# Attention and two expert layers: GpSimd makes part of the first operands, and a tile takes one reciprocal

## The chip, the core and the metric

The kernel runs on one core of one Trainium2 chip, as one program. The metric is the time of an execution on the device in microseconds (us). The engines are named as the profile names them: PE is TensorE (PEld its weight loads), DVE is VectorE, ACT is ScalarE, POOL is GpSimd, SP is SyncE, which here issues all the DMAs.

## What is computed

Local attention in chunks of 32 queries, then two layers of experts over the 1536 x 512 result. The first layer weighs its 4 experts by normalized `domain_probs`; the second weighs its 8 by gate logits that go through eight row and column normalizations.

```python
def _attn_ref(q, k, v, mem_k, mem_v):          # B, H, S, D = 2, 8, 768, 64
    for c in range(nc):                        # chunks of 32 queries
        k_full = np.concatenate([mem_k, k_ctx], axis=2)      # 8 + up to 56 keys
        scores = scale * np.matmul(q_c, k_full.transpose(0, 1, 3, 2))
        scores = scores - np.max(scores, axis=-1, keepdims=True)
        a = np.exp(scores)
        a = a / (np.sum(a, axis=-1, keepdims=True) + 1e-09)
        out[:, :, c_start:c_end] = np.matmul(a, v_full)

def _moe_ref(x, domain_probs, w1, w2):         # 1536 x 512, 4 experts of 1024
    for e in range(E):
        h = np.maximum(x @ w1[e], 0.0)
        out += p[:, e:e + 1] * (h @ w2[e])
# _moe2_ref: the same with 8 experts and the normalized gate table P
```

## The kernel before

**Tiles and operands.** Attention goes over 12 tiles of 128 tokens. The expert layers go over 36 units, an expert times a block of 512 tokens (`sb`, four tiles). Each matrix product is done by a scheme of seven products on half-size blocks (`PRODUCTS`: M1 to M7): the first operands are blocks A11, A12, A22 and combinations S1 to S4, the second ones B11, B21, B22 and T1 to T4. Every operand is kept as a pair of float16 halves, a high one (ACT converts) and a low one (DVE subtracts the high half from the source), and a product of 12 matmuls multiplies three pairs of halves.

**Where the work comes from.** `prepare` (L262) makes operands: it adds and subtracts 128 x 512 float32 sources on DVE (L299), has ACT convert to the high half (L307), and DVE make the low half (L311). `prep_w` (L323) loads four blocks of a weight and calls it; the first expert's weights are prepared as `w10`, `w11` (W1, groups 0 and 1) and `w20`, `w21` (W2) while attention runs, their sources lying in `raw`, `acc` and `h1` buffers. After every fourth attention tile `prepare` makes the operands `x0`, `x1`, `x2` of that block from the transposed output. `layer1` (L499) runs seven products, and DVE and ACT combine their results (L525, L531, L554) and make the operands h of the second layer: high halves on ACT (L539), low halves on DVE (L544 with the rectifier, L547 without). `layer2` (L571) runs seven products for each of two row groups and adds them into `acc` (L608, L612).

**An attention tile.** `scores` (L393): 32 small matmuls into two banks, one for each of two halves (`par`); DVE takes the maximum of each half (L419). In a wide tile DVE subtracts it (L424) and ACT takes one exponential of both halves (L440); in the two other tiles DVE scales the maximum (L421) and ACT takes eight exponentials with it as bias (L431). `weighted` (L443): transposes (L375), a copy by ACT (L381), 32 matmuls with the values, whose last column gives the sum; then for each half DVE adds 1e-9 (L469), takes the reciprocal (L470) and multiplies (L471); transposes again, and ACT copies into `raw`.

**What sets the order.** All operations are recorded in `Program` with the engine, an assumed cost and the keys that they read and write. `run` (L86) plays them through a list scheduler with these costs and due times (numbers in `PLAN`, L17), and emits every engine's instructions in the order found. Each engine then works strictly in that order and waits on semaphores. Where the planner sees PE idle early on, it puts filler matmuls (`warm`, L706). In the plan before, POOL has only the set-up of `ident` and `ones`.

Of the kernel before, what the change touches and what calls it, by code (L numbers as in the profile page):

```python
# [10 lines left out]
F32 = mybir.dt.float32  # L11
# [2 lines left out]
AX = mybir.AxisListType  # L14

P = 128
PLAN = dict(rf=(0.0, 4.0, 5.6, 18.0), wide=(0, 1, 2, 3, 4, 5, 7, 9, 10, 11), lead=27.37, step=6.0, pace=1.0, early=4.11, behind=3.0, tr=0.11, sm=0.04, margin=0.59, marg0=0.1, marga=0.12, margs=1.0, slack=1.13, slacka=0.35, slack0=0.29, mm=0.1088)  # L17


class Op:  # L20
# [154 lines left out]
def tile_attention_moe_moe(  # L175
# [52 lines left out]
    def f32t(tag, name="f"):  # L228
        return buf(tag, [P, 512], F32, name)
# [93 lines left out]
    def prep_w(which, e, g, src=None, temps=("T0", "T1"), force=None):  # L323
# [42 lines left out]
    def small(tag):  # L366
        return smt[tag]
# [25 lines left out]
    def scores(i):  # L393
# [19 lines left out]
        scale = 1.0 / float(D) ** 0.5  # L413
        eks = (f"{et}0", f"{et}1")
        wide = i in PLAN["wide"]
        for par in range(2):
            def mx(par=par):
                sm = small(st)
                nc.vector.tensor_reduce(out=sm[:, 0, :, par], in_=sb4(par), axis=AX.X, op=ALU.max)  # L419
                if not wide:  # L420
                    nc.vector.tensor_scalar_mul(sm[:, 0, :, par], sm[:, 0, :, par], -scale)  # L421

            def sub(par=par):
                nc.vector.tensor_tensor(  # L424
                    out=ex(et)[:, :, par, :], in0=sb4(par),
                    in1=small(st)[:, 0, :, par, None].to_broadcast([P, HP, 64]), op=ALU.subtract)

            def expf(par=par):
                sm = small(st)
                for hp in range(HP):  # L430
                    nc.scalar.activation(out=ex(et)[:, hp, par, :], in_=sb4(par)[:, hp, :], func=AF.Exp,  # L431
                                         scale=scale, bias=sm[:, 0, hp, par, None])

            pg.add("DVE", dve(256) + (0.0 if wide else 0.1), mx, (sc[par],), (f"{st}m{par}",))
            if wide:
                pg.add("DVE", dve(256), sub, (sc[par], f"{st}m{par}"), (eks[par],))
            else:
                pg.add("ACT", HP * 0.22, expf, (sc[par], f"{st}m{par}"), (eks[par],))
        if wide:
            pg.add("ACT", act(512, False), lambda: nc.scalar.activation(  # L440
                out=ex(et), in_=ex(et), func=AF.Exp, scale=scale), (), eks)

    def weighted(i, xdst):  # L443
        et, at, st = ee_t[i % 2], aT_t[i % 2], f"sm{i % 2}"
# [18 lines left out]
                            start=True, stop=True, skip_group_check=True)  # L463

        pg.add("PE", 32 * PLAN["sm"], go, (at, v0, v1), nb)
        for par in range(2):
            def norm(par=par):
                s = small(st)[:, 1, :, par]
                nc.vector.tensor_scalar_add(s, nb4(par)[:, :, D], 1e-9)  # L469
                nc.vector.reciprocal(s, s)  # L470
                nc.vector.tensor_tensor(  # L471
                    out=ex(et)[:, :, par, :], in0=nb4(par)[:, :, :D],
                    in1=s[:, :, None].to_broadcast([P, HP, D]), op=ALU.mult)

            pg.add("DVE", dve(256) + 0.2, norm, (nb[par],), (f"{st}s{par}", f"{et}{par}"))
# [22 lines left out]

    def layer1(sb, g, hs):  # L499
        bk = {"A": f"1A{blocks['1'] % 2 if blocks['1'] >= 4 else 0}", "B": "1B", "C": "1C"}  # L500
        blocks["1"] += 1
        last = {}
        for name, a, b, bb, first in PRODUCTS:
            bn, xt, wt = bk[bb], xtag(sb, a), f"w1{g}{b}"

# [28 lines left out]

        def hilo(o, s, rect):
            d = f"{hs}{o}"

            def hi():
                nc.scalar.activation(out=pair(d)[:, 0], in_=v2(f32t(s)), func=AF.Relu if rect else AF.Copy)  # L539

            def lo():
                t = pair(d)
                if rect:
                    nc.vector.scalar_tensor_tensor(out=t[:, 1], in0=v2(f32t(s)), scalar=0.0, in1=t[:, 0],  # L544
                                                   op0=ALU.max, op1=ALU.subtract)
# [198 lines left out]
    for gt in range(NT):  # L744
# [7 lines left out]
        if gt == 3:  # L752
            raw1 = [f"raw1{i}" for i in range(4)]
            h1 = [f"h1{o}" for o in OPA]
            prep_w(W1, 0, 0, raw1, force=PLAN["rf"][0])
            prep_w(W1, 0, 1, [f"acc{i}" for i in range(4)], ("acc4", "acc5"), force=PLAN["rf"][1])
            prep_w(W2, 0, 0, h1[:4], h1[4:6], force=PLAN["rf"][2])
            prep_w(W2, 0, 1, raw1, force=PLAN["rf"][3])
# [154 lines left out]
```

## Time and profile before

| | |
|---|---|
| Median of 3 runs | 1410.34 us (1410.24 to 1411.14) |
| The profiled execution | 1410.84 us |
| Its span, first to last instruction | 1409.1 us |
| PE busy | 1390.9 us, 99% |
| DVE busy | 1223.4 us, 87% |
| ACT busy | 720.6 us, 51% |
| POOL busy | 0.8 us |
| Mean granted TensorE clock | 0.999 of full speed |
| DMA | 71.47 MB, mean 51 GB/s |

The shares are means over the program. The attention stage and the preparation of the first operands lie in its first 130 us; the rest is the run of expert products. Matmuls are pipelined and their ends modelled, so a busy PE isn't PE at its peak, and the span on POOL is rough. A duration in the timeline includes the drain of an instruction, which the next one's start overlaps; the distance between starts is what an instruction costs its engine when they stand back to back.

### The profile page before, as it was taken

Reading aid. Unit: us, or ns where it says so; the run is one execution under the profiler, and the core shown is the slowest. Engines: PE = TensorE matmul, PEld = TensorE weight load, DVE = VectorE, ACT = ScalarE, POOL = GpSimd, SP = SyncE. Lnnn points to the kernel's source line nnn. Section 1 sums busy time; section 2 is a strip of 40 time slices with the busy share of each in tenths; the row PEclk is TensorE's granted clock in tenths of the full one; section 3 lists DMA queues with packets and bytes.
Section 4 is the critical chain, followed back from the end, with each engine's and each line's share of the span. In section 5 each row is a group of like instructions: output and inputs, shape, how many; then the busy total and the mean of one; then the engine's idle time right before and its main releaser. Section 6 shows DMA issues by size and latency. Waiting matters only on the chain.

```text
span 1409.1 us, 32996 instructions
## 1 busy us (share of the span) xinstructions
PE 1390.9 (99%) x14119; PEld 1244.0 (88%) x14119; DVE 1223.4 (87%) x2274; ACT 720.6 (51%) x1297; POOL 0.8 (0%) x7
## 2 busy tenths in 40 slices
PE   8899999999999999999999999999999999999998
PEld 8778888888889998888888888888888888888887
DVE  6998986996997999999899699699789789889874
ACT  4757564453554566556445445345356356445540
POOL 0000000000000000000000000000000000000000
PEclk9999999999999999999999999999999999999999
DMA  9620210120110111112012012012011111110001
GB/s 332 198 77 31 61 61 9 46 69 9 39 38 9 31 53 46 31 46 69 9 46 68 9 46 69 9 41 69 6 46 46 31 39 38 46 35 28 17 16 61
DMA packets 64819, 71.47 MB, mean 51 GB/s; under 512 B 6304, under 2 KB 55456, under 8 KB 64672
## 3 DMA queue, kind: packets, MB, share of 16 engines
q1 hardware_dynamic: 64672, 69.36, 15.8%
q8 instruction: 110, 1.80, 0.5%
q14 instruction: 37, 0.30, 0.1%
HBM read 66.20 MB, written 3.15 MB: 49 GB/s over the span
## 4 chain that ended last, share of the span: by engine, by line
PE 86%; DVE 11%; ACT 1%; issue 1%; DMA 0%; POOLq 0%; POOL 0%; SPq 0%; ACTq 0%
PE bank1A L493 24%; PE bank2A L493 24%; PE bank1C L493 12%; PE bank2C L493 12%; PE bank1B L493 6%; PE bank2B L493 6%; DVE t_f L525 1%; PE bank1A L706 1%; DVE b_f L554 1%; DVE raw_f L299 1%; DVE T_f L299 1%; DVE x2A_exp L471 1%; DVE h0S_op L547 0%; DVE acc_f L612 0%; DVE h0A_op L544 0%
## 5 line engine op out<-in xcount | busy, mean ns | idle before, releaser
L381 ACT ACTIVATE s_f<-bank1A 128x512 f32<-128x512 f32 x216 | 127.2, 589 | 258.1 <-PE bank1A L493 241.3
L493 PEld LDWEIGHTS <-w10T_op 128*128 128x128 f16 x1728 | 168.8, 98 | 22.3 <-issue 2.5
L493 PEld LDWEIGHTS <-w11T_op 128*128 128x128 f16 x1728 | 169.0, 98 | 20.0 <-issue 0.4
L493 PEld LDWEIGHTS <-w10B_op 128*128 128x128 f16 x1296 | 126.7, 98 | 15.5 <-issue 0.9
L493 PEld LDWEIGHTS <-w11B_op 128*128 128x128 f16 x1296 | 126.7, 98 | 15.5 <-issue 0.8
L493 PEld LDWEIGHTS <-h0S_op 128*128 128x128 f16 x1152 | 112.6, 98 | 14.4 <-issue 1.4
L493 PEld LDWEIGHTS <-h1S_op 128*128 128x128 f16 x1152 | 112.7, 98 | 13.1
L612 DVE SCALAR_TENSOR_TENSOR acc_f<-bank2A,pr,acc_f 128x256 f32<-128x256 f32 x168 | 80.8, 481 | 44.5 <-PE bank2A L493 44.5
L493 PEld LDWEIGHTS <-h2S_op 128*128 128x128 f16 x1104 | 108.0, 98 | 12.5
L525 DVE SCALAR_TENSOR_TENSOR t_f<-bank1C,s_f 128x512 f32<-128x512 f32 x144 | 98.7, 686 | 14.6 <-PE bank1C L493 13.3
L493 PEld LDWEIGHTS <-h0A_op 128*128 128x128 f16 x864 | 84.4, 98 | 10.1 <-issue 0.2
L493 PEld LDWEIGHTS <-h1A_op 128*128 128x128 f16 x864 | 84.5, 98 | 9.8
L493 PEld LDWEIGHTS <-h2A_op 128*128 128x128 f16 x828 | 81.0, 98 | 9.4
L539 ACT ACTIVATE h1A_op<-t_f 128x512 f16<-128x512 f32 x72 | 45.1, 629 | 59.3 <-DVE t_f L525 56.9
L539 ACT ACTIVATE h2A_op<-t_f 128x512 f16<-128x512 f32 x69 | 43.1, 625 | 30.2 <-DVE t_f L525 30.2
L539 ACT ACTIVATE h0A_op<-t_f 128x512 f16<-128x512 f32 x72 | 45.1, 629 | 24.0 <-DVE t_f L525 23.9
L612 DVE SCALAR_TENSOR_TENSOR acc_f<-bank2C,pr,acc_f 128x256 f32<-128x256 f32 x84 | 40.4, 481 | 19.2 <-PE bank2C L493 19.1
L544 DVE SCALAR_TENSOR_TENSOR h1A_op<-t_f,h1A_op 128x512 f16<-128x512 f32 x72 | 48.4, 687 | 7.8 <-ACT h1A_op L539 7.0
L525 DVE SCALAR_TENSOR_TENSOR t_f<-bank1B,s_f 128x512 f32<-128x512 f32 x72 | 49.4, 686 | 5.5 <-PE bank1B L493 5.3
L531 ACT ACTIVATE a_f<-bank1A 128x512 f32<-128x512 f32 x72 | 42.8, 594 | 20.5 <-PE bank1A L493 19.3
L554 DVE SCALAR_TENSOR_TENSOR b_f<-t_f,b_f 128x512 f32<-128x512 f32 x72 | 49.6, 689 | 1.7
L554 DVE SCALAR_TENSOR_TENSOR b_f<-t_f,a_f 128x512 f32<-128x512 f32 x72 | 49.4, 686 | 0.5 <-ACT a_f L531 0.5
(329 smaller groups left out, 3162.7 us busy)
## 6 DMA issues: line engine op xcount, KB each, us to landing
raw_f<-in_moe_w_dram SPq DMA_DIRECT2D x184, 256.0 KB, 2.8
out_dram<-acc_f SPq DMA_DIRECT2D x12, 256.0 KB, 2.0
acc_val<-in_v_dram SPq DMA_DIRECT2D x8, 260.0 KB, 5.2
h2A_val<-in_v_dram SPq DMA_DIRECT2D x8, 260.0 KB, 4.8
x2S_key<-in_k_dram SPq DMA_DIRECT2D x8, 256.0 KB, 4.8
acc_key<-in_k_dram SPq DMA_DIRECT2D x8, 256.0 KB, 4.9
h2S_val<-in_v_dram SPq DMA_DIRECT2D x6, 260.0 KB, 4.8
h2S_key<-in_k_dram SPq DMA_DIRECT2D x6, 256.0 KB, 5.3
```

The source lines that it names most:

```text
L299: nc.vector.tensor_tensor(out=f32t(o), in0=f32t(a), in1=f32t(b), op=alu)
L381: nc.scalar.activation(out=dst(), in_=src(), func=AF.Copy, scale=scale)
L471: nc.vector.tensor_tensor(out=ex(et)[:, :, par, :], in0=nb4(par)[:, :, :D], in1=s[:, :, None].to_broadcast([P, HP, D]), op=ALU.mult)
L493: nc.tensor.matmul(o, lhsT=l, rhs=r, start=st, stop=sp, skip_group_check=True)
L525: nc.vector.scalar_tensor_tensor(out=f32t(d), in0=bank[rb], scalar=CL1, in1=f32t(s), op0=ALU.mult, op1=ALU.add)
L531: nc.scalar.activation(out=f32t("a21"), in_=bank[bn], func=AF.Relu, scale=CL1)
L539: nc.scalar.activation(out=pair(d)[:, 0], in_=v2(f32t(s)), func=AF.Relu if rect else AF.Copy)
L544: nc.vector.scalar_tensor_tensor(out=t[:, 1], in0=v2(f32t(s)), scalar=0.0, in1=t[:, 0], op0=ALU.max, op1=ALU.subtract)
L554: nc.vector.scalar_tensor_tensor(out=f32t(o), in0=f32t(t), scalar=0.0, in1=f32t(s), op0=ALU.max, op1=alu, reverse1=rev)
L612: nc.vector.scalar_tensor_tensor(out=o, in0=s, scalar=sc, in1=o, op0=ALU.mult, op1=ALU.add)
L706: nc.tensor.matmul(bank["1A1"][:, :P], lhsT=ones, rhs=ones, start=True, stop=True)
```

## The change

- `prepare` takes an engine for its adds and one for its low halves. POOL makes the adds and subtracts for `w11`, `w20`, `w21`, `x0` and `x1`, and the low halves of `x1` and `x2`. For a low half on POOL `tensor_tensor` takes the place of `scalar_tensor_tensor` (the scale is 1 there). `layer1` gives POOL the low half of S4 in its blocks 0, 1, 2 and 6.
- The sums of both halves of an attention tile go into one small tile; one reciprocal over eight columns serves both, and the multiplication of each half waits for it.
- Both maxima of a tile share one key (`m`) of the planner, and in a tile that isn't wide one scaling serves both.
- The numbers in `PLAN` are others: which tiles are wide, when the weights are loaded, the lead of the first products, the margins.

```diff
-PLAN = dict(rf=(0.0, 4.0, 5.6, 18.0), wide=(0, 1, 2, 3, 4, 5, 7, 9, 10, 11), lead=27.37, step=6.0, pace=1.0, early=4.11, behind=3.0, tr=0.11, sm=0.04, margin=0.59, marg0=0.1, marga=0.12, margs=1.0, slack=1.13, slacka=0.35, slack0=0.29, mm=0.1088)
+PLAN = dict(rf=(0.0, 4.0, 42.7, 18.0), wide=(0, 1, 2, 4, 5, 6, 7, 8, 10, 11), lead=29.35, step=11.93, pace=1.0, early=3.15, behind=5.1, tr=0.11, sm=0.04, pw=(0, 1, 1, 1), px=((1, 0), (1, 1), (0, 1)), ph=((0, 'S4'), (1, 'S4'), (2, 'S4'), (6, 'S4')), margin=0.39, marg0=0.2, marga=0.07, margs=1.0, slack=1.15, slacka=0.43, slack0=0.3, mm=0.1088)
...
+def gps(n):
+    return 0.1 + n / 480.0
...
-    smt = {f"sm{i}": pool.tile([P, 2, HP, 2], F32, tag=f"sm{i}", name=f"sm{i}") for i in range(2)}
+    smt = {f"sm{i}": pool.tile([P, 2, 2, HP], F32, tag=f"sm{i}", name=f"sm{i}") for i in range(2)}
...
-    def prepare(dst, kind, scale, src, temps=("T0", "T1")):
+    def prepare(dst, kind, scale, src, temps=("T0", "T1"), adder="DVE", low="DVE"):
...
-                    nc.vector.tensor_tensor(out=f32t(o), in0=f32t(a), in1=f32t(b), op=alu)
-
-                pg.add("DVE", dve(512), go, (a, b), (o,))
+                    e = nc.gpsimd if adder == "POOL" else nc.vector
+                    e.tensor_tensor(out=f32t(o), in0=f32t(a), in1=f32t(b), op=alu)
+
+                pg.add(adder, gps(512) if adder == "POOL" else dve(512), go, (a, b), (o,))
...
+                    if low == "POOL":
+                        assert scale == 1.0
+                        nc.gpsimd.tensor_tensor(out=t[:, 1], in0=v2(f32t(s)), in1=t[:, 0], op=ALU.subtract)
+                        return
...
-                pg.add("DVE", dve(512), lo, (s, d + "h"), (d + "l",))
+                pg.add(low, gps(512) if low == "POOL" else dve(512), lo, (s, d + "h"), (d + "l",))
...
-                sm = small(st)
-                nc.vector.tensor_reduce(out=sm[:, 0, :, par], in_=sb4(par), axis=AX.X, op=ALU.max)
-                if not wide:
-                    nc.vector.tensor_scalar_mul(sm[:, 0, :, par], sm[:, 0, :, par], -scale)
+                m = small(st)[:, 0]
+                nc.vector.tensor_reduce(out=m[:, par], in_=sb4(par), axis=AX.X, op=ALU.max)
+                if par and not wide:
+                    nc.vector.tensor_scalar_mul(m, m, -scale)
...
-            pg.add("DVE", dve(256) + (0.0 if wide else 0.1), mx, (sc[par],), (f"{st}m{par}",))
+            pg.add("DVE", dve(256) + (0.0 if wide or not par else 0.1), mx, (sc[par],), (f"{st}m",))
             if wide:
-                pg.add("DVE", dve(256), sub, (sc[par], f"{st}m{par}"), (eks[par],))
...
+                pg.add("DVE", dve(256), sub, (sc[par], f"{st}m"), (eks[par],))
...
+        def recip():
+            r = small(st)[:, 1]
+            for par in range(2):
+                nc.vector.tensor_scalar_add(r[:, par], nb4(par)[:, :, D], 1e-9)
+            nc.vector.reciprocal(r, r)
+
+        pg.add("DVE", 0.3, recip, nb, (f"{st}s",))
...
+            pg.add("DVE", dve(256), norm, (nb[par], f"{st}s"), (f"{et}{par}",))
...
+            pool = not rect and (blk, o) in PLAN["ph"]
...
-                    nc.vector.tensor_tensor(out=t[:, 1], in0=v2(f32t(s)), in1=t[:, 0], op=ALU.subtract)
+                    e = nc.gpsimd if pool else nc.vector
+                    e.tensor_tensor(out=t[:, 1], in0=v2(f32t(s)), in1=t[:, 0], op=ALU.subtract)
...
+            adders = [("DVE", "POOL")[w] for w in PLAN["pw"]]
...
+                    *(("DVE", "POOL")[w] for w in PLAN["px"][gt // 4]))
```

The first place is an attention tile on DVE, ahead of x0's operands. Before, the maxima, subtractions and the normalization of two tiles stand so (`sm0`, `sm1` are the small tiles, banks 2B and 2C hold scores, 2A the weighted sums):

```order
L419 TENSOR_REDUCE sm0_81<-bank2B_69 128x4 [waits PE_49]
L419 TENSOR_REDUCE sm0_81<-bank2C_70 128x4 [waits PE_49]
L424 TENSOR_TENSOR x2A11_exp_164<-bank2B_69,sm0_81 128x4x64 [waits DVE_49]
L469 TENSOR_SCALAR sm1_82<-bank2A0_67 128x4 [waits PE_49]
L470 RECIPROCAL sm1_82<-sm1_82 128x4 [waits DVE_49]
L471 TENSOR_TENSOR x2A12_exp_265<-bank2A0_67,sm1_82 128x4x64 [waits DVE_49]
L469 TENSOR_SCALAR sm1_82<-bank2A1_68 128x4 [waits PE_49]
L470 RECIPROCAL sm1_82<-sm1_82 128x4 [waits DVE_49]
L471 TENSOR_TENSOR x2A12_exp_265<-bank2A1_68,sm1_82 128x4x64 [waits DVE_49]
L424 TENSOR_TENSOR x2A11_exp_164<-bank2C_70,sm0_81 128x4x64
```

In the changed order DVE has there:

```order
L429 TENSOR_REDUCE sm1_82<-bank2B_69 128x4 [waits PE_49]
L434 TENSOR_TENSOR x2A12_exp_213<-bank2B_69,sm1_82 128x4x64 [waits DVE_49,PE_49]
L429 TENSOR_REDUCE sm1_82<-bank2C_70 128x4
L434 TENSOR_TENSOR x2A12_exp_213<-bank2C_70,sm1_82 128x4x64 [waits DVE_49]
L320 SCALAR_TENSOR_TENSOR w11T3_op_612<-acc1_f_369,w11T3_op_612 128x512 [waits DMAHW7_49,Activation_49]
L480 TENSOR_SCALAR sm0_81<-bank2A0_67 128x4 [waits PE_49]
L480 TENSOR_SCALAR sm0_81<-bank2A1_68 128x4 [waits PE_49]
L481 RECIPROCAL sm0_81<-sm0_81 128x8 [waits DVE_49]
L486 TENSOR_TENSOR x2A11_exp_162<-bank2A0_67,sm0_81 128x4x64 [waits DVE_49,Activation_49]
L486 TENSOR_TENSOR x2A11_exp_162<-bank2A1_68,sm0_81 128x4x64
```

The second maximum has moved behind the first subtraction, and one reciprocal is gone.

The second place is the making of x1's operands and of `h1S4` (S4 of the h operand of the second group, from the buffer `t12`). Before, it stands on DVE:

```order
L554 SCALAR_TENSOR_TENSOR t12_f_1035<-t12_f_1035,b2_f_1097 128x512
L311 SCALAR_TENSOR_TENSOR w21B22_op_699<-raw13_f_159,w21B22_op_699 128x512
L299 TENSOR_TENSOR acc5_f_518<-raw02_f_582,raw03_f_588 128x512
L547 TENSOR_TENSOR h1S4_op_1648<-t12_f_1035,h1S4_op_1648 128x512 [waits Activation_49]
L299 TENSOR_TENSOR acc6_f_1667<-acc5_f_518,raw00_f_299 128x512 [waits DVE_49]
L311 SCALAR_TENSOR_TENSOR x1A12_op_1128<-raw01_f_302,x1A12_op_1128 128x512
L299 TENSOR_TENSOR raw01_f_302<-raw01_f_302,acc6_f_1667 128x512 [waits DVE_49]
```

In the changed order it stands on POOL, whose only rows behind the set-up are the 38 of the change:

```order
L304 TENSOR_TENSOR acc5_f_507<-raw02_f_582,raw03_f_584 128x512 [waits Activation_49]
L304 TENSOR_TENSOR acc6_f_1402<-acc5_f_507,raw00_f_308 128x512 [waits Pool_49]
L304 TENSOR_TENSOR raw01_f_313<-raw01_f_313,acc6_f_1402 128x512 [waits Pool_49]
L304 TENSOR_TENSOR raw02_f_582<-raw00_f_308,raw02_f_582 128x512
L318 TENSOR_TENSOR x1S4_op_1462<-raw01_f_313,x1S4_op_1462 128x512 [waits Activation_49]
L318 TENSOR_TENSOR x1S2_op_1465<-acc6_f_1402,x1S2_op_1465 128x512 [waits Activation_49]
L318 TENSOR_TENSOR x1S3_op_1508<-raw02_f_582,x1S3_op_1508 128x512 [waits Activation_49]
L318 TENSOR_TENSOR x1A22_op_1528<-raw03_f_584,x1A22_op_1528 128x512 [waits Activation_49]
L318 TENSOR_TENSOR x1S1_op_1533<-acc5_f_507,x1S1_op_1533 128x512 [waits Activation_49]
L564 TENSOR_TENSOR h1S4_op_1591<-t12_f_1100,h1S4_op_1591 128x512 [waits Activation_49]
```

`h1S4` has moved from the second place among x1's operations to the one behind nine of them, and PE's first load of it waits for POOL where it waited for DVE. From the third block of tokens on PE's products stand in the same order as before but for a few places.

## Rows read from the trace of the kernel before

**Rows 1.** The profile page: busy time, share and instructions of each engine, and the busy tenths in 40 equal slices of the span.

```profile
PE 1390.9 (99%) x14119; PEld 1244.0 (88%) x14119; DVE 1223.4 (87%) x2274; ACT 720.6 (51%) x1297; POOL 0.8 (0%) x7
...
PE   8899999999999999999999999999999999999998
...
POOL 0000000000000000000000000000000000000000
```

**Rows 2.** Busy time by stretch of the span, all engines; the columns are the stretch, its length, busy us and instructions (x) of PE, PEld, DVE, ACT and POOL, the granted clock, the DMA engines' busy share, and GB/s.

```profile
20.00:94.00 74.00, 65.38 (x1582) 56.30 (x1581) 71.73 (x171) 49.44 (x108) 0.00 (x0) 1.00 0.64 207
94.00:118.00 24.00, 23.99 (x330) 21.11 (x330) 19.36 (x46) 12.23 (x26) 0.00 (x0) 1.00 0.01 2
118.00:130.00 12.00, 10.93 (x154) 9.27 (x153) 11.55 (x23) 9.47 (x19) 0.00 (x0) 1.00 0.08 23
130.00:400.00 270.00, 270.00 (x2474) 241.85 (x2473) 235.11 (x413) 143.23 (x254) 0.00 (x0) 1.00 0.14 42
...
10.00:20.00 10.00, 7.59 (x166) 7.18 (x165) 7.03 (x17) 4.60 (x9) 0.00 (x0) 0.83 1.08 365
...
30.00:40.00 10.00, 8.87 (x246) 7.67 (x245) 9.76 (x27) 5.47 (x11) 0.00 (x0) 1.00 1.05 372
```

**Rows 3.** The stretch from 20 to 94 us by source line, in this order: 706 (PE and PEld), then on DVE 299, 311, 544, 547 and 554. The columns are as above, with only the engines that the line has.

```profile
20.00:94.00 74.00, 13.43 (x104) 12.15 (x103) 1.00 0.64 207
20.00:94.00 74.00, 12.57 (x19) 1.00 0.64 207
20.00:94.00 74.00, 21.63 (x34) 1.00 0.64 207
20.00:94.00 74.00, 4.01 (x6) 1.00 0.64 207
20.00:94.00 74.00, 5.37 (x8) 1.00 0.64 207
20.00:94.00 74.00, 5.38 (x8) 1.00 0.64 207
```

**Rows 4.** The chain of waits from 86 to 96 us, in order of time: start, us, engine, tile and line.

```profile
91.06 0.60 DVE acc_f L299
91.66 0.60 DVE h1S_op L547
92.26 0.61 DVE acc_f L299
...
92.90 0.63 ACT x1S_op L307
...
93.94 1.47 PE bank1A L493 x12
```

**Rows 5.** The timeline of PE: start, us, engine, line, operation, out<-in.

```profile
92.95 0.82 PE L493 MATMUL bank1C<-w21B_op,h1S_op 128*128 128x256 f16 x6
```

**Rows 6.** The timeline of DVE: a tile's normalization and three 512-column operations behind it, then the maxima of a tile that isn't wide and of a wide one.

```profile
22.85 0.15 DVE L469 TENSOR_SCALAR sm<-bank2A 128x4 f32<-128x4 f32 x1
23.04 0.18 DVE L470 RECIPROCAL sm<-sm 128x4 f32<-128x4 f32 x1
23.25 0.42 DVE L471 TENSOR_TENSOR x2A_exp<-bank2A,sm 128x256 f32<-128x256 f32 x1
23.59 0.15 DVE L469 TENSOR_SCALAR sm<-bank2A 128x4 f32<-128x4 f32 x1
...
24.33 1.28 DVE L311 SCALAR_TENSOR_TENSOR w10T_op<-raw_f,w10T_op 128x512 f16<-128x512 f32 x2
25.54 0.68 DVE L311 SCALAR_TENSOR_TENSOR w10T_op<-T_f,w10T_op 128x512 f16<-128x512 f32 x1
26.14 0.68 DVE L299 TENSOR_TENSOR acc_f<-acc_f 128x512 f32<-128x512 f32 x1
...
52.73 0.42 DVE L419 TENSOR_REDUCE sm<-bank2B 128x4 f32<-128x256 f32 x1
53.18 0.17 DVE L421 TENSOR_SCALAR sm<-sm 128x4 f32<-128x4 f32 x1
53.26 0.42 DVE L419 TENSOR_REDUCE sm<-bank2C 128x4 f32<-128x256 f32 x1
...
60.09 0.42 DVE L419 TENSOR_REDUCE sm<-bank2B 128x4 f32<-128x256 f32 x1
60.42 0.41 DVE L419 TENSOR_REDUCE sm<-bank2C 128x4 f32<-128x256 f32 x1
```

**Rows 7.** The timeline of DVE from 90.97 to 94 us.

```profile
90.97 0.68 DVE L299 TENSOR_TENSOR acc_f<-raw_f 128x512 f32<-128x512 f32 x1
...
92.18 0.69 DVE L299 TENSOR_TENSOR acc_f<-acc_f,raw_f 128x512 f32<-128x512 f32 x1
92.78 0.69 DVE L311 SCALAR_TENSOR_TENSOR x1A_op<-raw_f,x1A_op 128x512 f16<-128x512 f32 x1
93.50 0.69 DVE L299 TENSOR_TENSOR raw_f<-raw_f,acc_f 128x512 f32<-128x512 f32 x1
```

**Rows 8.** The timeline of POOL: the mask of `ident` in the set-up.

```profile
1.00 0.29 POOL masks.py:199 TENSOR_SCALAR_AFFINE_SELECT ident<-ident 128x128 f32<-128x128 f32 x1
```

**Rows 9.** The timeline of ACT: the copy of tile 7's output.

```profile
76.88 0.64 ACT L381 ACTIVATE raw_f<-bank1A 128x256 f32<-128x256 f32 x2
```

More of the change, by code (lines that the diff above doesn't have):

```diff
@@ L321, in raw_slot, with prep_w @@
         return [f"raw{r}{i}" for i in range(4)]
-    def prep_w(which, e, g, src=None, temps=("T0", "T1"), force=None):
+    def prep_w(which, e, g, src=None, temps=("T0", "T1"), force=None, adder="DVE"):
         src = src or raw_slot()
@@ L334, in prep_w @@
                     (), (tag,), 256 * 256 * 4, force=force)
-        prepare(lambda o: f"{name}{g}{o}", "B", SW, src, temps)
+        prepare(lambda o: f"{name}{g}{o}", "B", SW, src, temps, adder)
     def xtag(sb, o):
@@ L425, in sub @@
                     out=ex(et)[:, :, par, :], in0=sb4(par),
[L426 to L432, printed above, removed]
-            pg.add("DVE", dve(256) + (0.0 if wide else 0.1), mx, (sc[par],), (f"{st}m{par}",))
+                    in1=small(st)[:, 0, par, :, None].to_broadcast([P, HP, 64]), op=ALU.subtract)
+            pg.add("DVE", dve(256) + (0.0 if wide or not par else 0.1), mx, (sc[par],), (f"{st}m",))
             if wide:
-                pg.add("DVE", dve(256), sub, (sc[par], f"{st}m{par}"), (eks[par],))
-            else:
-                pg.add("ACT", HP * 0.22, expf, (sc[par], f"{st}m{par}"), (eks[par],))
+                pg.add("DVE", dve(256), sub, (sc[par], f"{st}m"), (eks[par],))
         if wide:
@@ L441, in scores, with expf @@
                 out=ex(et), in_=ex(et), func=AF.Exp, scale=scale), (), eks)
+        else:
+            for par in range(2):
+                def expf(par=par):
+                    for hp in range(HP):
+                        nc.scalar.activation(out=ex(et)[:, hp, par, :], in_=sb4(par)[:, hp, :], func=AF.Exp,
+                                             scale=scale, bias=small(st)[:, 0, par, hp, None])
+                pg.add("ACT", HP * 0.22, expf, (sc[par], f"{st}m"), (eks[par],))
     def weighted(i, xdst):
@@ L465, in weighted @@
         pg.add("PE", 32 * PLAN["sm"], go, (at, v0, v1), nb)
+        def recip():
+            r = small(st)[:, 1]
+            for par in range(2):
+                nc.vector.tensor_scalar_add(r[:, par], nb4(par)[:, :, D], 1e-9)
+            nc.vector.reciprocal(r, r)
+        pg.add("DVE", 0.3, recip, nb, (f"{st}s",))
         for par in range(2):
             def norm(par=par):
-                s = small(st)[:, 1, :, par]
-                nc.vector.tensor_scalar_add(s, nb4(par)[:, :, D], 1e-9)
-                nc.vector.reciprocal(s, s)
                 nc.vector.tensor_tensor(
                     out=ex(et)[:, :, par, :], in0=nb4(par)[:, :, :D],
-                    in1=s[:, :, None].to_broadcast([P, HP, D]), op=ALU.mult)
-            pg.add("DVE", dve(256) + 0.2, norm, (nb[par],), (f"{st}s{par}", f"{et}{par}"))
+                    in1=small(st)[:, 1, par, :, None].to_broadcast([P, HP, D]), op=ALU.mult)
+            pg.add("DVE", dve(256), norm, (nb[par], f"{st}s"), (f"{et}{par}",))
         transposes(xb, lambda hp: ex(et)[:, hp].rearrange("p a b -> p (a b)"), (f"{et}0", f"{et}1"))
@@ L500, in layer1 @@
         bk = {"A": f"1A{blocks['1'] % 2 if blocks['1'] >= 4 else 0}", "B": "1B", "C": "1C"}
+        blk = blocks["1"]
         blocks["1"] += 1
-        last = {}
         for name, a, b, bb, first in PRODUCTS:
@@ L546, in lo @@
                 else:
-                    nc.vector.tensor_tensor(out=t[:, 1], in0=v2(f32t(s)), in1=t[:, 0], op=ALU.subtract)
+                    e = nc.gpsimd if pool else nc.vector
+                    e.tensor_tensor(out=t[:, 1], in0=v2(f32t(s)), in1=t[:, 0], op=ALU.subtract)
             pg.add("ACT", act(512, False), hi, (s,), (d + "h",))
-            pg.add("DVE", dve(512), lo, (s, d + "h"), (d + "l",))
+            pg.add("POOL" if pool else "DVE", gps(512) if pool else dve(512), lo, (s, d + "h"), (d + "l",))
         def comb(o, t, s, alu, rev=False):
@@ L754, in tile_attention_moe_moe @@
             h1 = [f"h1{o}" for o in OPA]
[L755 to L758, printed above, removed]
+            adders = [("DVE", "POOL")[w] for w in PLAN["pw"]]
+            prep_w(W1, 0, 0, raw1, force=PLAN["rf"][0], adder=adders[0])
+            prep_w(W1, 0, 1, [f"acc{i}" for i in range(4)], ("acc4", "acc5"), force=PLAN["rf"][1], adder=adders[1])
+            prep_w(W2, 0, 0, h1[:4], h1[4:6], force=PLAN["rf"][2], adder=adders[2])
+            prep_w(W2, 0, 1, raw1, force=PLAN["rf"][3], adder=adders[3])
         if gt == 3:
@@ L764, in tile_attention_moe_moe @@
             prepare(lambda o, sb=gt // 4: xtag(sb, o), "A", 1.0, src,
-                    (("s1", "s2"), ("acc5", "acc6"), ("acc5", "acc6"))[gt // 4])
+                    (("s1", "s2"), ("acc5", "acc6"), ("acc5", "acc6"))[gt // 4],
+                    *(("DVE", "POOL")[w] for w in PLAN["px"][gt // 4]))
     release([f"acc{i}" for i in range(7)] + [f"h1{o}" for o in OPA])
```

## The prediction

> **What bounds the kernel now.** I read the busy shares and the forty slices first [rows 1]. PE is busy in nearly every slice, which says only that most of the program is a long run of products; POOL does nothing after its set-up. The busy times by stage [rows 2] divide the span: from 130 us on PE is busy all the time (270.00 of 270.00), and from 94 to 118 us as well; from 118 to 130 it misses 1.1 us. Anything to be won lies ahead of 94 us. There, from 20 to 94, PE is busy for 65.38 of 74.00 us, 13.43 of them with filler matmuls of line 706 [rows 3], so 74.00 - 65.38 + 13.43 = 22.1 us of PE go to nothing useful. DVE is busy for 71.73 of the 74.00. The chain of waits agrees: up to 92.9 us nearly every piece is DVE, and from 93.94 it is PE [rows 4]. What PE got last was `h1S4`, whose low half DVE made in the piece at 91.66 [rows 4]; PE began the matmuls with `h1S_op` at 92.95 [rows 5]. I call that product the milestone: **until it DVE sets the pace, behind it PE does**, and the steady part keeps PE's order of products almost untouched by the change. A milestone that comes earlier by some time therefore brings the end forward by the same time.
>
> **What leaves DVE.** In the changed order POOL has 38 operations on 512 columns: 20 combinations (adds and subtracts) for W1 group 1, W2 group 0 and 1, x0 and x1, 14 low halves of x1 and x2, and 4 low halves of S4. Back to back such an operation holds DVE for 0.60 us, whatever its line: starts at 24.33 (two, to 25.54), 25.54 and 26.14 [rows 6]. Of the 38, by the names and times of DVE's rows, 19 stood on DVE up to `h1S4` before: 16 for the weights and x0, the first combination of x1 (at 90.97 [rows 7]) and two S4. That is 19 x 0.60 = **11.4 us**. The other 19 ran behind it, three of them at once (92.18 to 93.50 [rows 7]), the rest from 94 us on, where DVE had time to spare (19.36 busy of 24.00 [rows 2]); they are costed at nothing, and PE's products hide them.
>
> **The one reciprocal.** A tile's normalization runs before from 22.85 to 24.33, 1.48 us: an add 0.19, a reciprocal 0.21, a multiply 0.34, and all three again [rows 6]. After: two adds in a row, one reciprocal over eight columns, two multiplies. A small operation that doesn't need its forerunner follows it after 0.08 (53.18 to 53.26 [rows 6]), so 0.08 + 0.19 + 0.21 + 0.34 + 0.34 = 1.16. Nine tiles reach this step ahead of the milestone: 9 x 0.32 = **2.9 us**.
>
> **What the change gives back.** The maxima of both halves now share one key, so the planner may not put the second maximum ahead of the first subtraction. The order becomes maximum, subtraction, maximum, subtraction, and each subtraction stands right behind the operation that it needs. Two independent maxima start 0.33 apart (60.09, 60.42), while the scaling that needs its maximum starts 0.45 behind it (52.73, 53.18) [rows 6]. There are 14 such pairs ahead of the milestone: 14 x 0.12 = **1.7 us** lost. In the two tiles that aren't wide one scaling is saved, and one maximum follows the other without a wait: from 0.53 per half (52.73 to 53.26) to 0.33 and 0.53, 2 x 0.2 = 0.4 us won. Together DVE has 11.4 + 2.9 - 1.7 + 0.4 = **13.0 us** less to do until the milestone.
>
> **What takes the place.** DVE will not be as full as before, since it now waits for others oftener. In 20 to 94 it idles 74.00 - 71.73 = 2.3 us; where it isn't the bound, from 94 to 130, it idles 24.00 + 12.00 - 19.36 - 11.55 = 5.1 of 36 [rows 2], which over the 61 us that the stage would then take is 9 us. So 0 to 6 us more idle time than before; I take **4**, nearer the upper end, because ACT (49.44 us in that stretch [rows 2]) then is at four fifths too and hands DVE all the high halves. DMA is full until 40 us (share 1.05 to 1.08 [rows 2]), which holds back the first tiles whatever DVE does; the same idle time pays for that.
>
> **What POOL costs.** No row has a two-input operation on POOL. The nearest is the mask of `ident`, 128 columns with one input, 0.29 us [rows 8]. If all of that were fixed, 512 columns would take 0.29; if all grows with the columns, 4 x 0.29 = 1.16; if a second input doubles it, 2.32. I take 1.16, as columns are what such work is made of, and keep 0.29 and 2.32 for the range. The 28 operations that the changed order puts ahead of `h1S4` on POOL are then 32.5 us, half of the stage, so POOL doesn't set its pace. What counts is its queue: the low half of `h1S4` stands behind nine x1 operations (four combinations, five low halves), and PE's first load of `h1S4` now waits for POOL. The x1 source of tile 7 was written at 76.88 before [rows 9]; brought forward by 7 to 8 us, to about 69, and with 10 x 1.16 = 11.6 behind it, `h1S4` is ready at about 81 to 82, plus 1.2 for the combination and conversion ahead of it, where PE wants it at 92.95 - 7 = 86. That leaves 3 us to spare at 1.16 and a delay of 8 to 9 us at 2.32. The x2 low halves (seven on POOL, the sixth of them the third x2 operand in PE's order) may cost PE about one more operation, 1.2 us, behind the milestone, against the 1.1 us that it misses from 118 to 130 now. For POOL's waits together I take **1.8 us** (0 to 8). Fewer fillers (55 entries in PE's order for 90) cost nothing: they are what PE does while it waits.
>
> **Sum.** 13.0 - 4 - 1.8 = 7.2 us, from the profiled execution's 1410.84 us to 1403.6. The median of the runs shown, 1410.34, is 0.5 below that execution, so **1403.1**.
>
> **Rival one, the other sign: POOL and DVE get in each other's way at SBUF.** Ahead of 94 us the lines whose both inputs lie in SBUF (299, 311, 544, 547, 554) make 12.57 + 21.63 + 4.01 + 5.37 + 5.38 = 49.0 of DVE's 71.73 us [rows 3]; without the 19 that leave (0.68 each) it is 36 of 59, 61%. Suppose that while POOL works on SBUF such a DVE operation stands still until POOL's ends. Three of five POOL operations then stop DVE for their whole length: 0.60 x 28 x 1.16 = 19.5 us. DVE gains 13.0 - 19.5 - 1.8 = -8.3, and -12.3 if the idle time comes on top: 1418.6 to 1422.6 from the median, say **1419**, since some of the stalls fall where DVE would idle anyway. It decides from 7.2 / 28 = 0.26 us of stall per POOL operation (no gain left), and from (7.2 + 2.8) / 28 = 0.36 it can be measured as slower. Against it: nothing in the trace, where POOL and DVE never work at once [rows 1, 8]; two fifths of DVE's work reads PSUM, and the runs of it (a tile's two maxima and subtractions, 1.33 us) are as long as a POOL operation. The Trainium skill, "SBUF — State Buffer", section "SBUF: two separate sides", speaks for it: VectorE and GpSimd share a pair of SBUF ports, an exclusive lock held for a whole instruction, which a VectorE instruction with two SBUF inputs needs against a GpSimd one that reads SBUF. By that rule in full the change is worth the 1419 above, by the rows alone the 1403.1. No run shown here has the case.
>
> **Rival two, no change.** The stalls are there but mostly fall under DVE's PSUM work (0.2 to 0.36 us each), or POOL takes 1.7 to 2.3 us an operation, so that 28 of them fill the stage and `h1S4` comes 4 to 8 us late. Either way 7 us are used up: about **1410**. **Rival three, all of the relief** reaches the end, with no new idle time: 1410.3 - 13.0 = 1397.3, so up to 1398, and lower if tiles also start sooner. That the change doesn't do what it says is ruled out by the orders: the 38 rows stand on POOL.
>
> **How the numbers follow.** Forecast, 1398 to 1407.5: 0.50. All of the relief, under 1398: 0.08. No change, 1407.5 to 1413.2: 0.17. Slower: 0.25, half of it above 1419. The range from 1396 to 1419 leaves out 0.05 below and 0.13 above. 0.2% is 2.8 us, about what a measurement can tell from no change: faster 0.50 + 0.08 = 0.58, same 0.17, slower 0.25.
>
> **What would show it.** In the profile after, the last filler and the point from which PE is busy all the time should lie near 86 to 88 us and not 94; DVE should be busy some 90% ahead of it; POOL's rows should be near 1.2 us and DVE's 512-column rows still 0.60 apart. DVE rows of 1 us and more beside POOL's, or idle time of DVE that ends with POOL, speak for rival one. A PE wait that POOL's line 564 ends speaks for rival two. The forecast is wrong if the 0.60 doesn't hold beside POOL.

## The result and the profile after

| kernel | median, us | range, us | ratio to before (95% interval) |
|---|---|---|---|
| before | 1410.29 | 1410.14 to 1411.14 | |
| changed | 1427.95 | 1427.59 to 1428.64 | 1.0125 (1.0107 to 1.0142) |

The changed kernel is 17.7 us slower; the forecast was 7.2 us faster. Its profiled execution has a span of 1426.2 us. The page's busy times and slices, to lay beside [rows 1]:

```profile
PE 1388.5 (97%) x14049; PEld 1238.1 (87%) x14049; DVE 1225.5 (86%) x2222; ACT 722.1 (51%) x1297; POOL 55.0 (4%) x45
...
PE   7779999999999999999999999999999999999999
...
POOL 1552000000000000000000000000000000000000
```

PE is below 9 tenths in the first three slices now, where it was in the first two, and POOL works in the first four. DVE has 52 instructions less than before and yet 2 us more of busy time. By stretch, in the columns of [rows 2]:

```profile
20.00:94.00 74.00, 54.22 (x1295) 44.09 (x1281) 70.67 (x128) 47.34 (x103) 35.55 (x25) 0.91 0.59 190
94.00:118.00 24.00, 19.17 (x281) 15.94 (x279) 16.25 (x33) 7.90 (x17) 6.28 (x5) 1.00 0.14 45
118.00:130.00 12.00, 12.00 (x168) 10.64 (x167) 7.25 (x17) 6.80 (x14) 0.24 (x1) 1.00 0.00 1
130.00:200.00 70.00, 65.80 (x650) 57.80 (x649) 63.08 (x100) 44.64 (x84) 11.26 (x9) 1.00 0.16 46
```

From 20 to 94 us DVE is as busy as before (70.67 for 71.73 us) but gets through 128 instructions in place of 171 (its order has 150 up to the point from which PE is busy). PE loses 4.83 us from 94 to 118 and 4.2 from 130 to 200, where it lost nothing. The point from which PE is busy has moved from 93.94 [rows 4] to 108.80, 14.9 us later; the chain of waits shows it (start, us, engine, tile, line):

```profile
102.64 0.60 DVE w21B_op L320
...
103.26 3.77 DMA raw_f<-in_moe_w_dram
...
107.06 0.69 DVE T_f L304
107.75 0.60 DVE raw_f L304
108.35 0.41 DVE acc_f L629
...
108.80 1.47 PE bank1C L508 x12
```

Where the time goes is seen in DVE's timeline (start, us, line, operation):

```profile
24.07 1.75 DVE L320 SCALAR_TENSOR_TENSOR w10B_op<-raw_f,w10B_op 128x512 f16<-128x512 f32 x1
25.74 1.75 DVE L304 TENSOR_TENSOR T_f<-raw_f,T_f 128x512 f32<-128x512 f32 x1
27.42 0.68 DVE L304 TENSOR_TENSOR raw_f<-raw_f 128x512 f32<-128x512 f32 x1
28.02 0.68 DVE L304 TENSOR_TENSOR raw_f<-raw_f,T_f 128x512 f32<-128x512 f32 x1
...
46.45 1.75 DVE L320 SCALAR_TENSOR_TENSOR x0S_op<-s_f,x0S_op 128x512 f16<-128x512 f32 x1
48.12 0.41 DVE L429 TENSOR_REDUCE sm<-bank2B 128x4 f32<-128x256 f32 x1
48.46 1.42 DVE L320 SCALAR_TENSOR_TENSOR x0S_op<-s_f,x0S_op 128x512 f16<-128x512 f32 x1
```

and in POOL's:

```profile
23.72 3.23 POOL L304 TENSOR_TENSOR acc_f<-acc_f 128x512 f32<-128x512 f32 x2 [0.19 <-DMA acc_f<-in_moe_w_dram]
...
43.02 1.27 POOL L304 TENSOR_TENSOR raw_f<-raw_f,s_f 128x512 f32<-128x512 f32 x1
44.26 1.72 POOL L304 TENSOR_TENSOR raw_f<-raw_f 128x512 f32<-128x512 f32 x1
45.94 1.71 POOL L304 TENSOR_TENSOR T_f<-raw_f 128x512 f32<-128x512 f32 x1
...
103.38 1.16 POOL L564 TENSOR_TENSOR h1S_op<-t_f,h1S_op 128x512 f16<-128x512 f32 x1 [4.00 <-ACT h1S_op L555]
```

Behind a DVE operation with both inputs in SBUF the next one starts after 0.60 us when POOL rests (27.42 to 28.02), as in [rows 6], and after 1.67 when POOL works (24.07 to 25.74). A maximum that reads PSUM (48.12) keeps its 0.41. POOL itself takes 1.16 to 1.29 us when DVE is elsewhere and 1.6 to 1.7 when they meet.

### The profile page after: what moved, and what is told of

It reads as the page before. It is cut to its first block, busy times and chain, and to the rows that moved or that the text cites. A ratio compares the mean times of both kernels' runs of the same rounds, so it can differ in the third digit from the quotient of the medians.

```text
span 1426.2 us, 32872 instructions
## 1 busy us (share of the span) xinstructions
PE 1388.5 (97%) x14049; PEld 1238.1 (87%) x14049; DVE 1225.5 (86%) x2222; ACT 722.1 (51%) x1297; POOL 55.0 (4%) x45
## 4 chain that ended last, share of the span: by engine, by line
PE 88%; DVE 9%; issue 1%; ACT 1%; DMA 0%; POOL 0%; DVEq 0%; POOLq 0%; ACTq 0%
PE bank1A L508 25%; PE bank2A L508 24%; PE bank1C L508 13%; PE bank2C L508 12%; PE bank1B L508 6%; PE bank2B L508 6%; DVE b_f L571 1%; DVE t_f L540 1%; PE bank1A L723 1%; DVE T_f L304 1%; DVE x2A_exp L486 0%; DVE w20B_op L320 0%; DVE raw_f L304 0%; DVE acc_f L629 0%; DVE h1S_op L564 0%
## 5 line engine op out<-in xcount | busy, mean ns | idle before, releaser
L508 PEld LDWEIGHTS <-w10B_op 128*128 128x128 f16 x1296 | 127.0, 98 | 16.2 <-issue 1.1
L508 PEld LDWEIGHTS <-h1S_op 128*128 128x128 f16 x1152 | 112.7, 98 | 16.2 <-DVE h1S_op L564 3.1
L555 ACT ACTIVATE h0A_op<-t_f 128x512 f16<-128x512 f32 x72 | 45.2, 629 | 23.3 <-DVE t_f L540 23.0
L629 DVE SCALAR_TENSOR_TENSOR acc_f<-bank2C,pr,acc_f 128x256 f32<-128x256 f32 x84 | 40.2, 478 | 17.7 <-PE bank2C L508 17.6
```

Of the source, the lines that this page charges most:

```text
L508: nc.tensor.matmul(o, lhsT=l, rhs=r, start=st, stop=sp, skip_group_check=True)
L629: nc.vector.scalar_tensor_tensor(out=o, in0=s, scalar=sc, in1=o, op0=ALU.mult, op1=ALU.add)
```

## The experiments

**Theory A:** while POOL reads SBUF, a DVE operation with two SBUF inputs stands still. **Theory B:** the loss comes from the new order: waits for POOL's queue, later loads, the new planning numbers. Beside each run the kernel before ran on the same chip; the differences are to its medians there, 1409.6 to 1410.2.

### Spare work on POOL beside the kernel before

Three kernels keep every row of before on PE, DVE, ACT and SP, and give POOL work on a buffer of its own, begun when W1's `acc3` has landed:

```diff
+    scr = pool.tile([P, 512], F32, tag="scr", name="scr")
...
+                if n == 0:
+                    nc.gpsimd.tensor_tensor(out=scr, in0=f32t("acc3"), in1=f32t("acc3"), op=ALU.add)
+                else:
+                    nc.gpsimd.tensor_tensor(out=scr, in0=scr, in1=scr, op=ALU.subtract)
```

> The kernel before, with all its orders on the other engines, and 38 subtractions of 128x512 on POOL beside it, from about 22 us on, on a buffer that nobody else uses; nobody waits for them. Theory A (while POOL reads SBUF, a DVE instruction with two SBUF inputs stands still, and the reverse): the changed kernel's trace has some 20.7 us of stretched DVE rows from 20 to 109 us for 28 POOL operations, 0.74 each; 38 of them before the milestone cost 38 x 0.74 = 28 us, up to 38 x 1.07 = 41 where every one alternates with a DVE row: 1436 to 1451 us, DVE's 0.68 us rows at 1.3 to 1.75 while POOL works. Theory B (the changed kernel is slow because of its new order: operations that wait for POOL's queue, weight loads that wait for POOL to let go of a buffer, later x1): no change, 1409 to 1412.

The others have `nc.gpsimd.tensor_scalar_mul(scr, scr, 0.5)` or `nc.gpsimd.memset(scr, 1.0)` in the last line.

> As the run with 38 spare subtractions, but POOL multiplies the spare buffer by a constant: one SBUF input. Theory A as it stands (POOL reading SBUF is enough): as slow as with two inputs for the POOL time that it takes, 1430 to 1451. Theory A in a narrower form (only a POOL operation with two inputs stands in DVE's way): 1409 to 1412. Theory B: 1409 to 1412.

> As the run with 38 spare subtractions, but 75 fills of the spare buffer with a constant, which read nothing. Theory A: no change, 1409 to 1412, and DVE's rows stay at 0.68. If any POOL access to SBUF stands in DVE's way: above 1420. Theory B: 1409 to 1412.

Measured (in brackets the ratio to the kernel before and its 95% interval, as everywhere below): two inputs **1433.22 us** (1.0159, 1.0144 to 1.0175), one input **1420.26** (1.0070, 1.0055 to 1.0085), fills **1409.90** (1.0000, 0.9990 to 1.0009). DVE's rows in the three, from 24 us on; the first group is of two inputs, the second of one, the third of fills:

```profile
26.97 1.52 DVE L323 SCALAR_TENSOR_TENSOR w10T_op<-T_f,w10T_op 128x512 f16<-128x512 f32 x1
28.42 1.52 DVE L311 TENSOR_TENSOR acc_f<-acc_f 128x512 f32<-128x512 f32 x1
```

```profile
25.44 1.10 DVE L323 SCALAR_TENSOR_TENSOR w10T_op<-T_f,w10T_op 128x512 f16<-128x512 f32 x1
26.46 0.68 DVE L311 TENSOR_TENSOR acc_f<-acc_f 128x512 f32<-128x512 f32 x1
```

```profile
26.07 0.69 DVE L323 SCALAR_TENSOR_TENSOR w10T_op<-T_f,w10T_op 128x512 f16<-128x512 f32 x1
26.67 0.68 DVE L311 TENSOR_TENSOR acc_f<-acc_f 128x512 f32<-128x512 f32 x1
```

Nobody waits for this work, so Theory B has no part in it: POOL's presence alone costs 23.2 us (0.61 per operation) with two inputs, 10.3 with one, nothing with fills. The first came out some 3 us below the range that A gave, 0.61 for 0.74; one input is less than half as dear, which neither form of A had. Set row against row beside the kernel before, 29 of DVE's 30 rows with two SBUF inputs are longer while POOL works with two inputs, by 22.2 us together; its 32 rows that read PSUM keep their length. Beside fills one such row is longer, next to the first POOL operation, which isn't a fill, and so are the two scalings of L421 (L433 in that run), with one SBUF input, 0.49 and 0.53 us in place of 0.17 [rows 6]; none of it reaches the end:

```profile
53.72 0.49 DVE L433 TENSOR_SCALAR sm<-sm 128x4 f32<-128x4 f32 x1
```

POOL's rows by line, duration min/median/max in ns, of the same three runs in turn:

```profile
L270 POOL TENSOR_TENSOR scr<-scr x37: 1038/1367/1548, 21.8 to 71.2; 128x512 f32<-128x512 f32 x37
```

```profile
L270 POOL TENSOR_SCALAR scr<-scr x37: 1487/1532/2042, 21.8 to 81.8; 128x512 f32<-128x512 f32 x37
```

```profile
L270 POOL MEMSET scr<- x75: 524/524/533, 21.6 to 64.7; 128x512 f32 x75
```

### The changed kernel with all of it back on DVE

```diff
-pw=(0, 1, 1, 1), px=((1, 0), (1, 1), (0, 1)), ph=((0, 'S4'), (1, 'S4'), (2, 'S4'), (6, 'S4'))
+pw=(0, 0, 0, 0), px=((0, 0), (0, 0), (0, 0)), ph=()
```

> The changed kernel with its 38 POOL operations given back to DVE; the one reciprocal, the shared key of the maxima and the new planning numbers stay. Theory A: the loss goes with POOL's operations; what stays is the 1.6 us of the narrow part of the sum and a new plan: 1405 to 1412. Theory B (new numbers and order): at least half of the loss stays, 1418 or more.

**1417.62 us** (1.0046, 1.0029 to 1.0062): a miss for A's range, and B's 1418 is within a hair. Taken alone it says that 7.6 of the 17.7 us are the new order. But the planner makes another order for DVE here, from numbers that go with the move; so the next run keeps the changed kernel's order itself.

### The changed kernel's order with fills on POOL

```diff
-                    nc.gpsimd.tensor_tensor(out=f32t(o), in0=f32t(a), in1=f32t(b), op=alu)
+                    nc.gpsimd.tensor_tensor(out=scr, in0=f32t(a)[:, :8], in1=f32t(b)[:, :8], op=alu)
+                    for _ in range(2):
+                        nc.gpsimd.memset(f32t(o), 0.0)
```

and likewise for the low halves.

> The changed kernel with the same orders on PE, DVE, ACT and SP, but each of POOL's 38 operations is replaced by a subtraction of 8 columns of the same inputs into a buffer of its own (so that POOL waits for the same things) and two fills of the whole target, 1.16 us together, which read nothing; the combinations and low halves are thus left out. Theory A (stalls of DVE beside POOL's reads): the fills left DVE's rows alone, so the relief of 13.0 us comes through, less the idle time and POOL's waits: 1398 to 1408. Theory B (the new order and numbers are the loss; DVE's own version of this order stood at 1417.6): 1415 or more. If both hold in part: between, and the difference to 1427.95 is the stalls.

**1404.22 us** (0.9960, 0.9945 to 0.9974). With rows that stand in the same order on every other engine and POOL busy for about the same time, the changed kernel is *faster* than before by 5.7 us; what POOL's reads add is 1427.95 - 1404.22 = **23.7 us** (23.4 if each is taken against the kernel before on its own chip). The stretch up to the point from which PE is busy, of this kernel and of the changed one:

```profile
20.00:90.64 70.64, 60.35 (x1453) 50.40 (x1454) 63.74 (x150) 51.48 (x114) 38.15 (x87) 0.98 0.66 213
```

```profile
20.00:108.80 88.80, 64.18 (x1435) 52.04 (x1421) 84.22 (x150) 52.58 (x114) 41.83 (x29) 0.92 0.53 170
```

DVE has 150 instructions in each: 63.74 us of them beside fills, 84.22 beside the real operations. 20.5 us are stretched rows, 2.3 of which only fill DVE's idle time (6.9 and 4.6 us); so the point moves by 18.2. Row against row, 21 of the 65 rows with two SBUF inputs are longer, by 18.6 us in duration; small rows with one SBUF input add 0.8, and the 70 that read PSUM keep theirs.

The two halves of this, split at the low half of `h1S4`:

> The changed kernel with its orders; the 29 POOL operations up to the low half of h1S4 are the 8-column subtraction and two fills (their combinations and low halves are left out), the nine behind it (x2 and two S4) are the real ones. If the stalls ahead of the milestone are nearly all of the loss, and those behind it the 4 us that PE misses from 130 to 200 us: 1404.2 + 4 = 1408, 1406 to 1410. If PE's products hide what happens behind the milestone, as the prediction had it: 1404 to 1406.

> The reverse: the 29 operations up to h1S4 are the real ones, and the nine behind it are the 8-column subtraction and two fills (their low halves are left out). If the stalls ahead are 20.7 us of DVE rows: 1404.2 + 20 = 1424, 1421 to 1426. If the stages share the loss otherwise, this and the run with the fills ahead still add up to 23.7 over 1404.2.

Fills ahead, real ones behind: **1409.41** (0.9993, 0.9984 to 1.0002), 5.2 us over the run with fills alone. The reverse: **1422.32** (1.0085, 1.0070 to 1.0100), 18.1 over it. Together 23.3 of the 23.7: the two parts add up. The nine operations behind the milestone cost 0.58 us each. DVE is nearly full there, above all from 118 to 130 us: it gets through 12 instructions in 11.40 of 12.00 us, where the run with fills alone had 19 in 11.74. Windows of the first and the second run:

```profile
118.00:130.00 12.00, 9.64 (x87) 8.19 (x85) 11.40 (x12) 8.14 (x16) 7.41 (x5) 1.00 0.22 68
130.00:200.00 70.00, 68.50 (x626) 60.99 (x624) 61.28 (x102) 44.32 (x83) 2.58 (x2) 1.00 0.18 56
```

```profile
118.00:130.00 12.00, 12.00 (x168) 10.69 (x166) 7.38 (x17) 7.39 (x15) 1.24 (x3) 1.00 0.01 1
130.00:200.00 70.00, 70.00 (x697) 62.39 (x696) 59.66 (x104) 46.63 (x89) 9.87 (x24) 1.00 0.17 50
```

### The parts of the change in the kernel before

The first of these takes the changed file, with before's planning numbers and softmax code; the second takes only `recip`, the two multiplies and the small tile's layout into before, the third all of the changed softmax code.

> The kernel before with its own planning numbers and its own softmax code, and the 38 operations on POOL. Theory A: 11.4 us of relief, against some 20 us of stalls up to the milestone and some 4 behind it: 1420 to 1428. Theory B (the new numbers and the shared key are the loss): 1400 to 1411.

> The kernel before, its own numbers, no POOL work: only the one reciprocal per tile; the keys of the two maxima stay apart. By the prediction's term, 9 tiles x 0.32 = 2.9 us less on DVE ahead of the milestone: 1407.4, 1404 to 1409. If the planner's new order takes it back (Theory B: any change of costs reshuffles the order): 1409 to 1414.

> As the run with the one reciprocal, and the shared key of the two maxima as well (all of the change's softmax code), before's numbers, no POOL work. By the prediction's terms 2.9 - 1.7 + 0.4 = 1.6 us less: 1408.7, 1.3 above the run with keys apart. Theory B: 1411 or more.

The move alone: **1425.54** (1.0105, 1.0088 to 1.0122), as A had it; B's explanation by the new numbers falls, since the loss comes with the old ones too. One reciprocal: **1408.96** (0.9994, 0.9984 to 1.0003). With the shared key: **1411.55** (1.0012, 1.0002 to 1.0021), 2.6 above it, where the terms had 1408.7 and Theory B 1411 or more. The normalization of the run with one reciprocal, and the maxima of the run with the shared key:

```profile
21.24 0.23 DVE L470 TENSOR_SCALAR sm<-bank2A 128x4 f32<-128x4 f32 x2 [0.66 <-PE bank2A L459]
21.51 0.20 DVE L471 RECIPROCAL sm<-sm 128x8 f32<-128x8 f32 x1
21.75 0.76 DVE L476 TENSOR_TENSOR x2A_exp<-bank2A,sm 128x256 f32<-128x256 f32 x2
22.42 0.68 DVE L311 SCALAR_TENSOR_TENSOR w10T_op<-raw_f,w10T_op 128x512 f16<-128x512 f32 x1
```

```profile
36.92 0.42 DVE L420 TENSOR_REDUCE sm<-bank2B 128x4 f32<-128x256 f32 x1
37.37 0.42 DVE L425 TENSOR_TENSOR x2A_exp<-bank2B,sm 128x256 f32<-128x256 f32 x1
37.71 0.41 DVE L420 TENSOR_REDUCE sm<-bank2C 128x4 f32<-128x256 f32 x1
```

A normalization takes 22.42 - 21.24 = 1.18 us (1.48 in [rows 6]), and a subtraction starts 0.45 behind its maximum: both terms of the sum were sized rightly as rows, though not in what they do to the time. Of nine times 0.30 only some 1.0 us reaches the end, which can't be told from none.

### Spare work where PE is the bound

Both take the 38 spare subtractions out of the first stage and begin them when `acc3` has its last product of the second expert's first unit, at 232.6 us (the first expectation puts that at 330, which was wrong). The second adds to each:

```diff
+                    for _ in range(8):
+                        nc.gpsimd.memset(scr, 1.0)
```

> The kernel before with its orders, and the 38 spare subtractions on POOL, but from about 330 us on, where PE is busy all the time and DVE 84 to 90%. Theory A (a stall costs time only where DVE is the bound): DVE's rows stretch as in the run from 22 us on, but the time stays within 3 us of the kernel before: 1409 to 1413. If a stalled DVE row holds up PE's banks wherever it stands: up to 38 x 0.61 = 23 us, 1433.

> The kernel before with its orders and the same 38 spare subtractions from about 232 us on, each but the first followed by eight fills (8 x 0.58 us), so that one comes every 6 us in place of every 1.4. If a stall costs what it exceeds of DVE's idle time in its stretch (in the dense run 38 stalls of up to 0.85 us are 32 us, against 55.00 - 48.81 = 6.2 us of idle time, and the run was 20.8 us longer): at 0.85 in 6 us against 14.6% of 6 = 0.87 the idle time nearly pays for it, 1409 to 1414. If every stalled DVE row costs PE wherever it stands: as the dense run, 1425 to 1433.

Dense: **1430.98** (1.0144, 1.0127 to 1.0161). Sparse: **1422.34** (1.0089, 1.0072 to 1.0106). Both went against the form of A that I gave them, that a stall is paid from DVE's idle time. The same stretch in the kernel before and in the dense run:

```profile
232.00:287.00 55.00, 55.00 (x506) 49.29 (x504) 48.81 (x85) 29.80 (x53) 0.00 (x0) 1.00 0.12 34
```

```profile
232.00:287.00 55.00, 39.46 (x324) 32.92 (x323) 52.78 (x54) 18.39 (x32) 50.66 (x38) 0.94 0.09 25
```

In the dense run that is arithmetic: 54 DVE instructions in place of 85, and PE starves. In the sparse one DVE's rows with two SBUF inputs are 16.2 us longer than in the kernel before, 0.43 us for each POOL operation against some 0.8 of idle time (DVE is busy 199.63 of the 230 us from 230 to 460 before), and still 12.7 us, 0.33 each, reach the end. PE's waits from 230 to 460 us there say where (engine, tile, line, releaser: us in total, times, longest):

```profile
PE bank2C L507 <- DVE acc_f L626: 3.7, 8, 0.7
PE bank1A L507 <- ACT s_f L395: 1.8, 2, 1.0
PE bank1C L507 <- DVE t_f L539: 1.6, 3, 0.9
```

PE needs a bank back from DVE every few products. A DVE row that comes late delays it at once, here by some 0.5 us on average and 0.9 at most, and idle time of DVE some products later doesn't give that back. In the kernel before, PE waits for nothing in this stretch; DVE's idle share there was no measure of how late its rows may come.

## Why the prediction was wrong

**The step that failed** is the choice between the forecast and rival one: that DVE's 512-column rows stay 0.60 apart beside POOL. Those with two SBUF inputs stand up to 1.67 apart. Rival one was priced and got 0.25; against it I held that no row of before showed the two engines at once, and that two fifths of DVE's work reads PSUM. The first is no evidence, only missing evidence; the second was in the price already (the 0.60 of 0.60 x 28 x 1.16 = 19.5 us) and was counted once more in the chance. Its stall term was right in size: 20.5 us measured up to the milestone. Its parts were not quite: 17 stalls of 1.16 in the term, 21 longer rows with some 0.9 each in the trace. The Trainium skill's rule that I named there ("SBUF — State Buffer", "SBUF: two separate sides") names the case that decided, and the runs agree with both its sides: 23.2 us lost beside POOL work with two SBUF inputs, none beside fills, which the rule leaves out since they read nothing.

**The range** failed by a second step, "costed at nothing, and PE's products hide them", of the 19 operations behind the milestone. Nine of them on POOL cost 5.2 us: the stage from 118 to 200 us has the same clash. Rival one had no term for it, so even its 1418.6 to 1422.6 ends below 1427.95.

**What held and what didn't.** Without the stalls the sum comes near: 5.7 us faster with fills, 7.2 in the sum. Part of that is luck, since only 3.3 of the 5.7 come where the sum had all of them, ahead of the milestone. Inside it:
- The new idle time of DVE: 4 us taken, 6.9 - 2.3 = 4.6 with fills.
- POOL's time of 1.16: 1.16 undisturbed for a low half (103.38), 1.27 for a combination. That it came out so is luck: it was four times a row with one input, and with one input 512 columns take 1.49 us or more, longer than with two.
- POOL's waits, 1.8 us: none show. Behind the set-up no wait of PE ends with POOL, neither with fills nor in the changed kernel.
- The relief of 13.0 us: DVE's busy time up to the milestone falls by only 71.73 - 63.74 = 8.0, counted from 20 us. The order brings other work into that stretch: seven 512-column rows of the first expert's weights, which before stood ahead of 20 us (DVE is busy 8.45 us there before and 5.91 with fills), and `T_f` of the next expert's weights, for whose load DVE waits in its queue (the DMA piece at 103.26 in the chain; with fills one of 3.21 us stands there as well). So the milestone is 3.3 us earlier; the other 2.4 us of the 5.7 come behind it, 1.1 of them from 118 to 130, where PE no longer misses what it did in [rows 2]. Where the last 1.3 come from wasn't settled.
- The shared key with the scaling that it saves, 1.7 - 0.4 = 1.3 us: 2.6 by the two runs. The one reciprocal, 2.9 us: 1.0. Together they lose some 1.6 us against the kernel before, where the sum had 1.6 won.

**What stays open.** With all work back on DVE the new numbers stand 6.1 us above the same softmax code with the old ones (1417.62 and 1411.55). Which of the numbers does it wasn't tried, and it isn't what made the change slow: with the old numbers the move costs 15.6 us. The lower granted clock from 20 to 94 us (0.91 in the mean, so in part 1.2 GHz in place of 2.4) isn't it either. Its lowest stretch, 40 to 50 us at 0.66, comes behind two in which PE was busy for 7.37 and 7.77 of 10 us, and it has the same 0.66 with all on DVE, while POOL rests. A slower PE could put the milestone off by letting DVE wait, and DVE waits less in the changed kernel (4.6 us) than with fills (6.9 us, at 0.98).

No run beat the kernel before with the work done in full; the one reciprocal with keys apart is within the measurement of it.

## What to carry to other kernels

Moving a two-input operation from DVE to POOL took 0.60 us off DVE and put 0.6 to 1.07 us of standstill on it wherever both worked on SBUF: before such a move, count DVE's operations with two SBUF inputs beside it. Of the work tried on POOL only fills cost no time, and of DVE's rows only those that read PSUM kept their length beside all of it (but for one small row, 0.40 us for 0.16 beside one input). An average idle share of the other engine is no reserve where a third engine needs each of its results at once, as PE's banks here. And when a price is missing from the trace, work that nobody waits for, put beside the unchanged program, measures it by itself.

## What was not expected of the hardware

- POOL with one SBUF input holds DVE up for 0.42 us (rows of 1.10 and 0.68 in turn), though its own operation is longer (1.53 us median, 1.04 at the least for the subtraction of the spare buffer from itself). The Trainium skill, in the section named above, has whoever starts first hold the ports for its whole instruction; here the measurement decides: the standstill is well short of the POOL row.
- The price goes with the inputs too: 1.67 - 0.60 = 1.07 us beside a combination of two buffers, 28.42 - 26.97 - 0.60 = 0.85 beside the subtraction of one buffer from itself.
- The two don't always take turns. In the sparse run one POOL operation stood for 3.72 us while DVE's rows with two SBUF inputs went on 0.60 apart (POOL's row, then DVE's):

```profile
433.08 3.72 POOL L270 TENSOR_TENSOR scr<-scr 128x512 f32<-128x512 f32 x1
```

```profile
433.42 0.68 DVE L313 TENSOR_TENSOR raw_f<-raw_f,T_f 128x512 f32<-128x512 f32 x1
434.02 0.68 DVE L558 SCALAR_TENSOR_TENSOR h2A_op<-t_f,h2A_op 128x512 f16<-128x512 f32 x1
434.62 0.68 DVE L325 SCALAR_TENSOR_TENSOR w20T_op<-raw_f,w20T_op 128x512 f16<-128x512 f32 x1
```
